# Who issues the eight V weight pieces of a memory-attention kernel, SyncE or ScalarE, with a newly searched instruction order

## The chip, the cores and the metric

The kernel runs on one core of a Trainium2 chip. Its time is device time in microseconds (us) from launch to end; runs of one kernel are compared by their median. A difference is written as after minus before, so a positive number means slower. The engines are TensorE (PE), VectorE (DVE), ScalarE (ACT), GpSimd (POOL) and SyncE (SP); SP, ACT and POOL can each issue DMAs.

## The reference

Four layers run one after another on 2048 tokens of width 512, in bfloat16: attention with memory, a gated feed-forward layer, and both once more, each behind a layer norm and added to its input. The attention walks over 64 segments of 32 tokens. Eight memory rows stand ahead of each segment, and the first eight output rows of a segment are the memory of the next, so that segments form a chain.

```python
for s in range(n_seg):                      # 64 segments of 32 tokens
    h = concat([mem, x[:, s*32:(s+1)*32]])  # 8 + 32 rows, 512 wide
    q, k, v = h @ Wq, h @ Wk, h @ Wv        # 32 heads of 128
    p = softmax(mask(q k^T * scale))
    o = (p v) @ Wo
    mem, out = o[:, :8], o[:, 8:]
x = x + attention(layernorm(x))
x = x + (sigmoid(xn w_gate) * (xn w_up)) w_down
# both lines a second time with the same weights
```

## The kernel before

**Stages.** `Kern.trace` records the whole kernel as tasks. A step (`emit_step`) handles one segment of the first attention layer together with the segment six steps earlier of the second, 70 steps in all; a block is four segments. V does not depend on the chain except for the memory rows, so it is computed ahead for whole blocks (`v_group`, `v_pass`, `v_half`, `v_strip`): a token block of x is loaded (`load_x`), normalised on VectorE with one power function on GpSimd (`layernorm_T`), transposed on TensorE (L595), copied to a tile `xvf` or `xvl` by ScalarE or VectorE, and multiplied by the V weights `wv_sb` (L635, L673, L762). The product is copied from PSUM to SBUF (L1228 on ScalarE, L1230 on VectorE) and written by a DMA to a scratch tensor `scr` in HBM, from which each step reads its V rows back (`vsb`).

**The start.** While the weights of 16 MB are on their way, TensorE does V work for the first blocks. The V weights come in eight pieces of 512 KB (`load_weights`, L511), one for each four heads; then the pieces of `wq_sb`, `wk_sb` and `wo_sb`, between which stand the loads of x and the writes to `scr`. Until the first transposed block is there, TensorE runs filler products on a tile `hot` (L1214), which are part of no result.

**The order.** The string `SEQUENCE` holds a packed order of all tasks and, for each task that two engines may do, the engine. `Planner.plan` unpacks it, and `replay` walks through it with estimated durations, from which it picks buffers, the number of filler products and the place up to which TensorE must have come before a large feed-forward weight load is issued (`pace`). Within each engine the instructions then stand in that order, and each waits by semaphores for what it needs.

**What the V pieces wait for, before.** All eight are issued by SyncE. A piece carries a dependency on the piece two ahead of it (`tk.after`), so that two are under way at a time. Apart from that the framework beneath gives each DMA of SyncE (and of ScalarE) one of eight semaphores in turn, here called lanes; a DMA that takes a lane waits until the DMA that had it last has landed.

Of the kernel before, what the change touches and what calls it, by code (L numbers as in the profile page):

```python
# [1293 lines left out]
```

## Time and profile before

| what | value |
|---|---|
| timed runs | 1745.2, 1745.24, 1746.65 us; median 1745.24 us |
| profiled execution, first to last instruction | 1747.1 us |
| TensorE busy | 1733.4 us (99%) |
| VectorE, ScalarE, GpSimd busy | 1248.4, 1128.5, 859.0 us |
| DMA, mean | 156 GB/s, 273.41 MB |
| chain that ended last | TensorE 94%, DMA 3% |

The span of the profiled execution, its own time, lies 1.9 us (0.1%) above the median of the timed runs; the page shows no time around it. A difference that is worked out in the trace is therefore put on the median as it is. On the page, the idle time of an engine counts only where the chain of waits passes through it; TensorE is busy nearly throughout, so what can change the time is where TensorE stands idle or runs filler, and that is at the two ends.

### The profile page before, as it was taken

To read this page: it belongs to the slowest core of one execution; us is meant where nothing else is said; L and a number is where in the kernel's file an instruction comes from. 1 tells how busy PE (TensorE), PEld (TensorE's weight loads), DVE (VectorE), ACT (ScalarE), POOL (GpSimd) and SP (SyncE) were. 2 spreads that over 40 slices of the span, in tenths; PEclk is the share of its full clock that TensorE was granted. 3 is DMA by queue.
4 is the path that set the end of the run, shared out by engine and by line. 5 is a ranking of instruction groups with operands and counts; after the bars stand their busy time and mean duration, and the time that the engine had idled before them with its cause. 6 is when DMAs were issued, how large, how long until landed. Compare 5 with 4: busy or idle time off the path is not lost.

```text
span 1747.1 us, 91842 instructions
## 1 busy us (share of the span) xinstructions
PE 1733.4 (99%) x39162; PEld 1491.8 (85%) x39162; DVE 1248.4 (71%) x4208; ACT 1128.5 (65%) x3119; POOL 859.0 (49%) x1367
## 2 busy tenths in 40 slices
PE   9999999999999999999999999999999999999998
PEld 4688789889898988989888888989888888988886
DVE  5677777677767776786777767776777776767676
ACT  3576777566666766666666666666665666666564
POOL 5624345635544554445445554544455364454543
PEclk9999999999999999999999999999999999999999
DMA  8935355645645555545555464545455464554644
GB/s 285 320 100 155 109 151 161 195 113 153 174 130 163 156 159 143 165 125 164 152 148 158 136 184 128 166 138 153 132 174 166 139 174 128 144 156 131 178 120 134
DMA packets 145583, 273.41 MB, mean 156 GB/s; under 512 B 39686, under 2 KB 86018, under 8 KB 145174
## 3 DMA queue, kind: packets, MB, share of 16 engines
q0 software_dynamic: 72944, 198.79, 39.8%
q1 hardware_dynamic: 72230, 68.75, 13.3%
q8 instruction: 307, 5.03, 1.2%
q14 instruction: 102, 0.84, 0.2%
HBM read 221.78 MB, written 27.07 MB: 142 GB/s over the span
## 4 chain that ended last, share of the span: by engine, by line
PE 94%; DMA 3%; DVE 1%; SPq 1%; issue 1%; POOL 0%; ACT 0%; POOLq 0%; ACTq 0%
PE bank L868 34%; PE bank L995 17%; PE bank L1097 12%; PE bank L762 8%; PE bank L635 6%; PE bank L1120 6%; PE bank L904 4%; PE bank L976 4%; PE bank L950 2%; PE bank L595 1%; PE bank L1214 1%; DMA wk_sb<-in_A_Wk_dram 1%; DMA wo_sb<-in_A_Wo_dram 0%; PE bank L1065 0%; DMA scr<-wu 0%
## 5 line engine op out<-in xcount | busy, mean ns | idle before, releaser
L868 PE MATMUL bank<-hT,wq_sb 128*128 128x80 bf16 (+3 forms) x8960 | 616.4, 198 | 1.0 <-DVE hT L1008 0.3
L868 PE MATMUL bank<-hT,wk_sb 128*128 128x80 bf16 (+3 forms) x8960 | 616.3, 198 | 0.8 <-DMA wk_sb<-in_A_Wk_dram 0.6
L1228 ACT CAST qku<-bank 128x480 bf16<-128x480 f32 (+4 forms) x770 | 384.7, 508 | 223.7 <-PE bank L868 194.6
L868 PEld LDWEIGHTS <-wq_sb 128*128 128x128 bf16 x8960 | 454.2, 99 | 32.1 <-issue 15.1
L868 PEld LDWEIGHTS <-wk_sb 128*128 128x128 bf16 x8960 | 446.9, 99 | 1.1 <-DMA wk_sb<-in_A_Wk_dram 0.7
L995 PE MATMUL bank<-otsb,wo_sb 128*128 128x80 bf16 (+1 forms) x8960 | 360.2, 198 | 2.2 <-DMA wo_sb<-in_A_Wo_dram 1.3
L918 DVE TENSOR_TENSOR st<-bank,cst 40x240 f32<-40x240 f32 (+3 forms) x768 | 280.5, 368 | 113.2 <-PE bank L904 97.5
L995 PEld LDWEIGHTS <-wo_sb 128*128 128x128 bf16 x8960 | 336.6, 99 | 15.5 <-DMA wo_sb<-in_A_Wo_dram 2.0
L1228 ACT CAST otsb<-bank 128x480 bf16<-128x480 f32 (+3 forms) x420 | 200.2, 483 | 83.4 <-PE bank L976 52.8
L1090 POOL DMA_DIRECT2D wu<-in_B_w_up_dram x217 | 166.5, 768 | 170.0 <-PE bank L950 36.4
L1114 POOL DMA_DIRECT2D wd<-in_B_w_down_dram x217 | 156.9, 723 | 182.0 <-PE bank L1120 39.6
L1224 POOL DMA_DIRECT2D vsb<-sst x351 | 178.2, 512 | 129.6 <-ACT sst L1228 64.7
L1089 POOL DMA_DIRECT2D wg<-in_B_w_gate_dram x217 | 166.4, 767 | 138.1 <-PE bank L1097 56.7
L928 ACT ACTIVATE st<-st 80x240 f32<-80x240 f32 (+3 forms) x420 | 159.2, 381 | 58.0 <-DVE st L925 54.8
L1097 PE MATMUL bank<-xnT,wg 128*128 128x128 bf16 (+2 forms) x1784 | 171.5, 218 | 0.0
L1097 PE MATMUL bank<-xnT,wu 128*128 128x128 bf16 (+2 forms) x1784 | 171.1, 218 | 0.0
L930 DVE TENSOR_REDUCE small<-st 80x6 f32<-80x240 f32 (+3 forms) x420 | 151.5, 363 | 23.4 <-ACT st L928 20.2
L1220 ACT ACTIVATE ptsb<-bank,small 120x160 bf16<-120x160 bf16 (+3 forms) x430 | 156.6, 386 | 17.2 <-PE bank L950 10.7
L904 PE MATMUL bank<-qku 128*128 128x80 bf16 (+1 forms) x2240 | 162.7, 197 | 1.0 <-issue 0.9
L925 DVE TENSOR_TENSOR st<-st,small 80x240 f32<-80x240 f32 (+3 forms) x420 | 155.0, 370 | 5.7
L939 DVE TENSOR_TENSOR pb<-st,small 80x240 bf16<-80x240 f32 (+3 forms) x420 | 154.1, 370 | 5.7
L923 DVE TENSOR_REDUCE small<-st 80x6 f32<-80x240 f32 (+3 forms) x420 | 152.5, 364 | 6.2
(108 smaller groups left out, 2554.1 us busy)
## 6 DMA issues: line engine op xcount, KB each, us to landing
wg<-in_B_w_gate_dram POOLq DMA_DIRECT2D x220, 256.0 KB, 4.2
wu<-in_B_w_up_dram POOLq DMA_DIRECT2D x220, 256.0 KB, 4.2
wd<-in_B_w_down_dram POOLq DMA_DIRECT2D x220, 256.0 KB, 3.9
vsb<-scr SPq DMA_DIRECT2D x137, 66.0 KB
scr<-vst SPq DMA_DIRECT2D x90, 96.0 KB
vsb<-scr POOLq DMA_DIRECT2D x93, 66.0 KB, 3.4
vsb<-sst SPq DMA_DIRECT2D x179, 32.0 KB
vsb<-sst POOLq DMA_DIRECT2D x169, 32.0 KB, 2.8
```

What stands on the lines that cost most here:

```text
L868: nc.tensor.matmul(o_ap, lhsT=W[:, c, h * P:(h + 1) * P], rhs=mv(c), start=(c == 0), stop=(c == DC - 1))
L904: nc.tensor.matmul(s_all(SB)[:, w0 + i, :], lhsT=fview(qku[:, i, 0, 0:1], [(1, P)]), rhs=qku[:, i, 1, 0:ncol], start=True, stop=True)
L918: pl.add("DVE", dve_ns(n, True), lambda gsz=gsz, hs=hs, st=st, SB=SB, pj_=pj_, npj_=npj_, mk=mk, idx=idx: nc.vector.tensor_tensor(out=st[p ...
L928: pl.add("ACT", act_ns(n), lambda hs=hs, st=st: nc.scalar.activation(out=st[pr, hs], in_=st[pr, hs], func=ACTF.Exp, scale=self.scale), r=s ...
L995: nc.tensor.matmul(WB[:, c * ncol:(c + 1) * ncol], lhsT=self.wo[:, h, c * P:(c + 1) * P], rhs=otsb[:, hl, 0:ncol], start=(h == 0 and c == ...
L1089: pl.add("POOL", 760, lambda wg=wg, fs=fs: nc.gpsimd.dma_start(out=wg[:], in_=self.wgv[:, :, fs]), r=[("wo", self.H - 1)], w=[gk] + bt, la ...
L1090: pl.add("POOL", 760, lambda wu=wu, fs=fs: nc.gpsimd.dma_start(out=wu[:], in_=self.wuv[:, :, fs]), r=[("wo", self.H - 1)], w=[uk] + bt, la ...
L1097: nc.tensor.matmul(gu[:, 2 * i + k, 0:n], lhsT=W[:, c, i * P:(i + 1) * P], rhs=xnT[:, c, rw], start=(c == 0), stop=(c == DC - 1))
L1114: pl.add("POOL", 760, lambda wd=wd, ip=ip: nc.gpsimd.dma_start(out=wd[:], in_=self.wdv[:, 2 * ip:2 * ip + 2, :]), w=[dk] + (["boot"] if se ...
L1220: nc.scalar.activation(out=dst, in_=src, func=ACTF.Copy, scale=by)
L1224: {"SP": nc.sync, "POOL": nc.gpsimd}[tk.on].dma_start(out=got[1], in_=got[2])
L1228: nc.scalar.copy(out=dst, in_=src)
```

## The change

- The V weight pieces, and the pieces of Wq, Wk and Wo, may be issued by SyncE or by ScalarE; a bit in the packed order says which. In the order given, ScalarE issues all eight V pieces, ahead of its table load, and one piece each of Wk and Wq later.
- The dependency of a V piece on the piece two ahead of it is gone.
- The planner's estimate of transfers has a separate bus for each issuing engine, eight lanes for SyncE and eight for ScalarE, other constants, and a table load of 1240 ns before ScalarE's first computing task.
- `SEQUENCE` is another order of the whole kernel. TensorE's products are the same in number apart from the filler (58 filler products before, 56 after; the first batch 23 before, 18 after).

```diff
-    BUS, BUS0, SLOW, BIG, ROOM, TAIL = 345.0, 290.0, 18000.0, 300000, 1.0, 1200.0
-    LEAD = {"SP": 1000.0, "POOL": 1800.0}
-    FIRST = {"PE": 0.0, "ACT": 2040.0, "DVE": 980.0, "POOL": 3500.0, "SP": 750.0}
+    BUS, BUS0, SLOW, BIG, ROOM, TAIL = 335.0, 304.0, 20400.0, 300000, 1.0, 1850.0
+    TAILP, CP, STEAL, FIX = 1000.0, 142.0, 0.4, 12400.0
+    LEAD = {"SP": 600.0, "ACT": 600.0, "POOL": 2800.0}
+    FIRST = {"PE": 0.0, "ACT": 800.0, "DVE": 980.0, "POOL": 3500.0, "SP": 750.0}
+    TABLE = 1240.0
...
+            if e == "ACT" and not tk.nb and not table:
+                table, t = True, max(t, free[e] + self.TABLE)
...
-            if e == "SP":
-                lanes.append(tk.done)
-                if len(lanes) >= 8:
-                    free[e] = max(end, lanes[-8])
+            if e == "SP" or e == "ACT" and tk.nb:
+                lanes[e].append(tk.done)
+                if len(lanes[e]) >= 8:
+                    free[e] = max(end, lanes[e][-8])
...
-        def ld(dst, src, nb, keys, after=()):
-            return pl.add("SP", 480, lambda: nc.sync.dma_start(out=dst, in_=src), r=after, w=keys, boost=self.boot(), lat=1750.0, nb=nb)
+        def ld(dst, src, nb, keys, after=(), engs=("SP", "ACT")):
+            return pl.add(engs, {e: 480 for e in engs}, lambda: ("dma", dst, src), r=after, w=keys, boost=self.boot(), lat=1750.0, nb=nb)
...
-            tk = ld(self.wv[:, :, cs], wv_v[:, :, cs], P * self.DC * n * P * 2, [("wv", h) for h in range(h0, h0 + n)], [("wv", h0 - 8)] if h0 > 4 else [])
-            if h0 > 4:
-                tk.after = pl.writer[("wv", h0 - 8)]
+            ld(self.wv[:, :, cs], wv_v[:, :, cs], P * self.DC * n * P * 2, [("wv", h) for h in range(h0, h0 + n)])
...
-                    {"SP": nc.sync, "POOL": nc.gpsimd}[tk.on].dma_start(out=got[1], in_=got[2])
+                    {"SP": nc.sync, "ACT": nc.scalar, "POOL": nc.gpsimd}[tk.on].dma_start(out=got[1], in_=got[2])
```

In the built program the first DMAs of the two issuing engines stand as follows, in program order, each with its lane and with the DMA whose landing it waits for (the lanes go round over both engines' DMAs together):

```
 1 ACT wv piece 1   lane 0                     13 ACT wv piece 5   lane 4, waits for 5
 2 SP  x (xs3)      lane 1                     14 SP  mask 3 KB    lane 5, waits for 6
 3 SP  x (xs4)      lane 2                     15 ACT wv piece 6   lane 6, waits for 7
 4 SP  x (hff)      lane 3                     16 SP  mem0 8 KB    lane 7, waits for 8
 5 SP  x (xs0)      lane 4                     17 SP  x (xa1)      lane 0, waits for 9
 6 ACT wv piece 2   lane 5                     18 SP  x (xs1)      lane 1, waits for 10
 7 SP  x (xs2)      lane 6                     19 ACT wv piece 7   lane 2, waits for 11
 8 SP  x (xa0)      lane 7                     20 SP  wq 393 KB    lane 3, waits for 12
 9 SP  x (xs5)      lane 0, waits for 1        21 SP  x (oxT)      lane 4, waits for 13
10 ACT wv piece 3   lane 1, waits for 2        22 ACT wv piece 8   lane 5, waits for 14
11 SP  x (oxT)      lane 2, waits for 3        23 SP  x (xs3)      lane 6, waits for 15
12 ACT wv piece 4   lane 3, waits for 4        24 SP  x (hff)      lane 7, waits for 16
```

After its eighth piece ScalarE's stream goes on with the table load, then the copies of the first two transposed blocks to `xvf` (two copies, both on ScalarE; before, one of the two was VectorE's), for which the first V product waits.

208 lines of the change are left out of this document (110 added, 98 removed).

## The prediction

> **What bounds the kernel now.** I read the page first, then a table of stretches, then the timeline of TensorE with the waits ahead of its rows, and last the queue of SyncE at the start. The page:
>
> ```profile
> span 1747.1 us, 91842 instructions
> PE 1733.4 (99%) x39162; PEld 1491.8 (85%) x39162; DVE 1248.4 (71%) x4208; ACT 1128.5 (65%) x3119; POOL 859.0 (49%) x1367
> ```
>
> TensorE is idle for only 13.7 us. Where those lie says the table of stretches (length, then busy time of PE, PEld, DVE, ACT and POOL, then granted clock, DMA share, GB/s):
>
> ```profile
> core 0: us, PE busy (x) PEld busy (x) DVE busy (x) ACT busy (x) POOL busy (x), PEclk, DMA share, GB/s
> 0.00:10.00 10.00, 8.94 (x36) 3.71 (x36) 4.04 (x12) 1.59 (x2) 3.65 (x19) 1.00 0.70 214
> 10.00:20.00 10.00, 10.00 (x54) 4.67 (x52) 6.76 (x19) 4.06 (x8) 5.95 (x14) 1.00 0.87 283
> 20.00:40.00 20.00, 17.64 (x119) 8.04 (x118) 11.26 (x28) 7.72 (x19) 12.75 (x25) 1.00 0.93 311
> 40.00:60.00 20.00, 19.79 (x310) 11.67 (x309) 10.90 (x34) 9.25 (x24) 15.06 (x29) 1.00 1.02 373
> 60.00:80.00 20.00, 18.12 (x324) 11.95 (x320) 12.53 (x42) 11.96 (x40) 8.83 (x18) 1.00 0.97 310
> 100.00:1700.00 1600.00, 1597.06 (x36638) 1401.08 (x36635) 1159.64 (x3925) 1056.84 (x2897) 784.22 (x1218) 1.00 0.53 150
> 1700.00:1747.00 47.00, 41.88 (x1089) 33.61 (x1085) 30.39 (x106) 22.33 (x79) 19.12 (x28) 1.00 0.47 134
> ```
>
> From 100 to 1700 us TensorE misses 2.9 us. No new order can win more than that there, and the end has 5.1 us idle, most of it the last additions and the output's landing. So the first 80 us decide; there the DMA engines are nearly full and TensorE waits for weights. TensorE's timeline (start, length, row; in brackets the idle time ahead and what ended it):
>
> ```profile
> 1.06 7.77 PE L1214 MATMUL bank<-hot 128*128 128x512 bf16 x23 [1.06 <-DVE cst L484]
> 8.67 0.39 PE L595 MATMUL bank<-cst,xn 128*128 128x128 bf16 x4
> 9.50 0.76 PE L1214 MATMUL bank<-hot 128*128 128x512 bf16 x3
> 10.23 2.76 PE L635 MATMUL bank<-wv_sb,xvf 128*128 128x512 bf16 x12
> 20.79 2.76 PE L635 MATMUL bank<-wv_sb,xvf 128*128 128x512 bf16 x12 [0.45 <-DMA wv_sb<-in_A_Wv_dram]
> 25.69 1.04 PE L635 MATMUL bank<-wv_sb,xvf 128*128 128x512 bf16 x4 [1.91 <-DMA wv_sb<-in_A_Wv_dram]
> 57.05 0.27 PE L868 MATMUL bank<-hT,wq_sb 128*128 128x54 bf16 x4 [0.21 <-DMA wq_sb<-in_A_Wq_dram]
> 62.06 0.27 PE L868 MATMUL bank<-hT,wk_sb 128*128 128x54 bf16 x4 [0.56 <-DMA wk_sb<-in_A_Wk_dram]
> 68.99 0.47 PE L995 MATMUL bank<-otsb,wo_sb 128*128 128x40 bf16 x12 [0.22 <-DMA wo_sb<-in_A_Wo_dram]
> 77.49 0.47 PE L995 MATMUL bank<-otsb,wo_sb 128*128 128x40 bf16 x12 [0.49 <-DMA wo_sb<-in_A_Wo_dram]
> 78.58 0.84 PE L995 MATMUL bank<-otsb,wo_sb 128*128 128x40 bf16 x20 [0.62 <-DMA wo_sb<-in_A_Wo_dram]
> ```
>
> The first V product starts at 10.23. Two waits for V pieces cost 0.45 + 1.91 = 2.36 us, five for the later weights 0.21 + 0.56 + 0.22 + 0.49 + 0.62 = 2.10 us. After that TensorE is full, so what the start loses or wins goes through to the end. SyncE's queue and its neighbours show why the pieces are late:
>
> ```profile
> 0.81 0.46 SPq L511 DMA_DIRECT2D wv_sb<-in_A_Wv_dram  x1
> 1.33 0.96 SPq L724 DMA_DIRECT2D xs<-in_A_x_dram  x2
> 2.34 0.43 SPq L511 DMA_DIRECT2D wv_sb<-in_A_Wv_dram  x1
> 4.51 0.38 SPq L511 DMA_DIRECT2D wv_sb<-in_A_Wv_dram  x1
> 8.59 0.40 SPq L511 DMA_DIRECT2D wv_sb<-in_A_Wv_dram  x1
> 18.17 0.40 SPq L511 DMA_DIRECT2D wv_sb<-in_A_Wv_dram  x1
> ```
>
> The third piece is issued when the first has landed (4.51), the fourth when the second has (8.59), and the eighth only at 18.17.
>
> **The waits that are left.** The change takes out the dependency between pieces, but the built program still has a wait ahead of six of the eight: the lanes go round over the DMAs of SyncE and ScalarE together, while the planner counts eight for each. Pieces 3 to 7 wait for x blocks. Piece 8 waits for the small mask copy, which SyncE issues only when piece 2 has landed. ScalarE works in order, so its table load and the copies of the first transposed blocks stand behind all of that:
>
> ```profile
> 0.81 1.28 ACT L1228 ACT_TABLE_LOAD   x1 [0.81 <-PEq L1275]
> 9.70 0.48 ACT L1228 COPY xvf<-bank 128x384 bf16<-128x384 bf16 x1 [7.61 <-PE bank L595]
> 4.86 0.69 DVE L582 BATCH_NORM_STATS2 small<-xs 128x6 f32<-128x512 bf16 x1 [3.85 <-DMA xs<-in_A_x_dram]
> ```
>
> **Term 1, the first V product.** Piece 2 now has six x blocks and piece 1 beside or ahead of it: 6 x 0.13 + 2 x 0.52 = 1.84 MB. At the 214 GB/s of the first ten microseconds this is down at 8.6. From 4.51, when 0.52 MB was down, to 8.59, when 1.31 MB was, the rate was 0.79 / 4.08 = 193 GB/s; this gives 4.51 + 1.32 / 0.193 = 11.3. I take 9.9, the middle. Then the mask copy. No row shows it; the nearest are small transfers of GpSimd's queue, in the whole run and in the first 80 us (KB, median us to landing):
>
> ```profile
> vsb<-sst POOLq DMA_DIRECT2D x169, 32.0 KB, 2.8
> vsb<-scr POOLq DMA_DIRECT2D x5, 16.0 KB, 5.3
> ```
>
> I take 3.2, near the lower one, because SyncE's queue then holds only two x blocks ahead of it. Then come piece 8's issue (0.40), the table load (1.28), the copy of 0.48, the second copy (a third as large, some 0.3 with its start) and some 0.1 of handing over: 2.6 us. So the first V product starts at 9.9 + 3.2 + 2.6 = 15.7, between 8.6 + 2.8 + 2.6 = 14.0 and 11.3 + 5.3 + 2.6 = 19.2. Against 10.23 that is **+5.5 us** (+3.8 to +9.0). Nothing covers it: TensorE works in order, and behind these products stands everything else. The earlier x (six blocks ahead of most V pieces; the first one was waited for until 4.86) gives nothing, since the transposed blocks then wait for ScalarE.
>
> **Term 2, the clock.** With 5 fillers fewer in the first batch (18 for 23, so about 1 us less) the last filler ends near 9 where it now ends at 10.2, and TensorE then stands idle for nearly 7 us. What that does to it these rows show: fillers at the start, and the end of the run.
>
> ```profile
> 1.06:6.50 5.44, 5.44 (x13) 1.90 (x14) 1.00 0.80 240
> 6.57:8.83 2.26, 2.26 (x11) 0.88 (x9) 1.00 0.94 324
> 1743.60:1747.30 3.70, 0.06 (x1) 0.00 (x0) 0.70 (x1) 0.00 (x0) 0.00 (x0) 1.00 0.13 35
> 1747.30:1749.00 1.70, 0.00 (x0) 0.00 (x0) 0.00 (x0) 0.00 (x0) 0.00 (x0) 0.51 0.00 0
> ```
>
> The first 13 fillers take 5.44 us (0.42 each), the next 11 2.26 us (0.21 each): a cold start costs 13 x 0.21 = 2.7 us. After TensorE's last product the granted clock stays 1.00 for 3.7 us and is then 0.51. An idle time of 7 us is longer than that, so I count a second cold start, **+2.7 us** (0 if the clock holds, 2.7 at the most as the rows go). The Trainium skill, "TensorE: Matmul & The Clock Gate", part 1 on the HAM clock gate, says that a window of about 3.4 us without work halves the clock and that a busy window of that length restores it; the trace agrees on the first (3.7 us). By the page's window the restart would cost half of 3.4, 1.7 us, an estimate from that page, and the sum 1 us less; the measured 5.44 us decide.
>
> **Term 3, the two V waits.** From 15.7 on the pieces lie ready: the last is issued near 13.5 and in the trace of before a piece takes 3.7 to 7.5 us to land (0.81 to 4.51, 18.17 to 25.69), so by 21, while the built order asks for it only after some 12 us of V products. **-2.4 us.** If a piece still is late, part of it stays.
>
> **Term 4, the later weights.** The built order puts SyncE's first write of V results behind 13 us of V products and its last before the big weight pieces behind 19 us. Ahead of the first stand 6.3 MB, down near 22 us at the 214 and 283 GB/s of the table. So the transfers pause until the V results come, at 15.7 + 2.7 + 13 = 31 us, and run freely from 15.7 + 2.7 + 17 = 35.4 on. From there 15.1 MB remain up to the last piece of `wo_sb`: at 373 GB/s 40.5 us, at 310 GB/s 48.7 us, so until 76 to 84. TensorE asks for that piece after 60 us of products, which by the idle-free pace of before takes 61.4 us: at 79.8. So TensorE waits 0 to 4 us there, beside 2.10 now. I take the 2.1 again: **0** (-2.1 to +2.3).
>
> The rest of the order (steps, feed-forward loads, end) I cost at nothing: 2.9 us of idle time in 1600 leave nothing to take, and the built order asks for the feed-forward weights at least 5.7 us of products after their release, before 5.9. That cover gone, some tenths of a microsecond each time; I allow 1.5 us either way.
>
> **Sum.** 5.5 + 2.7 - 2.4 + 0 = +5.8 us. The span of the profiled execution would go from 1747.1 to 1752.9, the median from 1745.24 to **1751.0 us**.
>
> **Rivals.** (a) *It does what it says*: the pieces leave back to back. Then ScalarE is done with them at 0.81 + 8 x 0.4 = 4.0 and with its table at 5.3, long before the first copy. With the x blocks ahead the second lands about 1 us sooner, the first V product starts near 9.3 (-0.9), and the waits of 2.36 and 2.10 go: -5.4 us, 1739.9 us. It decides if piece 2 and the mask copy are down before about 6 us. For it speaks that the DMA share was 0.70 and 0.87 in the first 20 us, room for about 1 MB more; against it the waits in the built program. The Trainium skill, "DMA: Bandwidth & Descriptors", section "Issuing engines are not separate DMA queues", says that issuing from several engines saves only issue time, which speaks against this rival; no run here shows it yet. (b) *The late start is absorbed*: the first V product at the lower end, 14.0 (+3.8), a cold start of 2.7, -2.4, and the 2.1 of later waits gone because the weights get ahead: +2.0, 1747.2 us. (c) *The transfers become the bound*: the upper ends of terms 1 and 4, 9.0 + 2.7 - 2.4 + 2.3 = +11.6, 1756.8 us; the share of 1.02 from 40 to 60 us speaks for it.
>
> **How the numbers follow.** The median of three runs tells about 0.2%, 3.5 us, from no change. The forecast has 0.55, (a) 0.10, (b) 0.23, (c) 0.12. Faster is (a) alone: 0.10. Within 0.2% (to 1748.7) are most of (b) and the lower edge of the forecast: 0.25. Slower: 0.65. The forecast's own range is 1747.5 to 1754.5. The range for 8 in 10 leaves out (a) and the upper part of (c): 1744 to 1756.
>
> **What would show it.** In the trace after: ScalarE's table load starts near 13.5 instead of 0.81; the third and later V pieces have gaps between them; TensorE is idle from about 9 to 15.7; the first V products are 0.43 us apart and later 0.21; no waits for `wv_sb`; waits of about 2 us for `wk_sb` and `wo_sb` before 85 us. A table load before 6 us, or a first V product before 11, makes the prediction wrong at term 1; products at full speed after the pause, at term 2; TensorE idle time in 100 to 1700 us far from 3 us, in what I costed at nothing.

## The result, and the profile after

| | runs | median, us | lowest to highest |
|---|---|---|---|
| before | 6 | 1745.9 | 1744.1 to 1751.54 |
| after | 6 | 1757.32 | 1755.54 to 1758.42 |

After is slower by a factor of 1.0061 (95% interval 1.005 to 1.0072), which is 10.6 us (8.7 to 12.6). The forecast was slower by 5.8 us, 1751.0 us, between 1744 and 1756; the measured median lies 1.3 us above that range. The profiled execution of after took 1755.54 us, its span is 1753.7 us. (One execution further down, of the run e16, took 2863.2 us at a granted clock of 0.556; it is left out of that run's median and ratio.) From the page of after:

```profile
span 1753.7 us, 91577 instructions
PE 1721.8 (98%) x38946; PEld 1492.5 (85%) x39160; DVE 1256.8 (72%) x4187; ACT 1139.6 (65%) x3140; POOL 874.6 (50%) x1407
```

TensorE seems to have lost 12 us of busy time, but it shows 38946 products for 39160 weight loads: some 200 records of products are missing in this trace. A second profile of the same kernel (the run e10 below) has them from 100 to 1700 us; there TensorE is busy for 1597.45 of 1600 us, where before has 1597.06:

```profile
100.00:1700.00 1600.00, 1597.45 (x36668) 1402.71 (x36665) 1165.64 (x3900) 1069.23 (x2922) 795.91 (x1251) 1.00 0.53 150
```

So in that execution the loss is ahead of 100 us. The table of stretches of after (columns as in the prediction):

```profile
10.00:20.00 10.00, 4.06 (x10) 1.45 (x11) 3.44 (x11) 2.53 (x4) 1.54 (x3) 0.66 1.10 345
20.00:30.00 10.00, 9.95 (x56) 4.90 (x56) 6.36 (x18) 5.76 (x17) 3.91 (x8) 1.00 0.21 66
40.00:80.00 40.00, 35.29 (x475) 20.32 (x478) 22.49 (x66) 17.29 (x49) 29.87 (x56) 1.00 0.98 339
```

From 10 to 20 us TensorE works 4.06 us, at a granted clock of 0.66. From 20 to 30 us the DMA engines all but stop (share 0.21, 66 GB/s); before has them full there:

```profile
20.00:30.00 10.00, 7.64 (x64) 3.30 (x63) 5.63 (x15) 4.83 (x11) 5.10 (x11) 1.00 1.01 342
```

From 40 to 80 us TensorE stands idle for 4.7 us (2.1 in before). Its timeline in after names the causes:

```profile
8.47 0.54 PE L1228 MATMUL bank<-hot 128*128 128x512 bf16 x2
15.94 4.67 PE L649 MATMUL bank<-wv_sb,xvf 128*128 128x512 bf16 x12 [6.92 <-ACT xvf L1242]
20.44 0.61 PE L609 MATMUL bank<-cst,xn 128*128 128x128 bf16 x8
49.58 0.27 PE L882 MATMUL bank<-hT,wq_sb 128*128 128x54 bf16 x4 [0.71 <-DMA wq_sb<-in_A_Wq_dram]
56.46 0.27 PE L882 MATMUL bank<-hT,wk_sb 128*128 128x54 bf16 x4 [0.63 <-DMA wk_sb<-in_A_Wk_dram]
61.61 0.28 PE L882 MATMUL bank<-hT,wk_sb 128*128 128x54 bf16 x4 [1.18 <-DMA wk_sb<-in_A_Wk_dram]
67.03 0.27 PE L882 MATMUL bank<-hT,wq_sb 128*128 128x54 bf16 x4 [1.39 <-DMA wq_sb<-in_A_Wq_dram]
70.15 0.27 PE L882 MATMUL bank<-hT,wk_sb 128*128 128x54 bf16 x4 [0.53 <-DMA wk_sb<-in_A_Wk_dram]
```

The first V product starts at 15.94, after 6.92 us without work, and waits for ScalarE's copy `xvf`. The twelve products take 20.44 - 15.94 = 4.50 us; with the clock at full speed they take 2.60 (from 9.90 to 12.50 in e1 below). No wait for `wv_sb` is left; five waits for `wq_sb` and `wk_sb` make 4.44 us. ScalarE's queue, and two rows of SyncE's:

```profile
0.81 12.94 ACTq L1238 DMA_DIRECT2D wv_sb<-in_A_Wv_dram  x8
13.77 1.28 ACT L1242 ACT_TABLE_LOAD   x1 [13.77 <-DMA wv_sb<-in_A_Wv_dram]
15.07 0.82 ACT L1242 COPY xvf<-bank 128x384 bf16<-128x384 bf16 x2
```

```profile
7.78 0.92 SPq L509 DMA_DIRECT2D cst<-cst  x1
31.53 1.41 SPq L1238 DMA_DIRECT2D scr<-wu  x2
```

The eight pieces occupy ScalarE's queue from 0.81 to 13.75, not back to back; the last is issued at 13.37, when the mask copy, issued at 7.78, has landed (13.35). Then come the table load and the two copies. SyncE's first write of V results, behind which the next weights of its queue stand, leaves at 31.53. Up to 40 us after has issued three pieces of `wq_sb` and `wk_sb`, before seven.

### The profile page after: what moved, and what is told of

It is laid out like the page before. It is cut to its first block, busy times and chain, and to the rows that moved or that the text cites. A ratio compares the mean times of both kernels' runs of the same rounds, so it can differ in the third digit from the quotient of the medians.

```text
span 1753.7 us, 91577 instructions
## 1 busy us (share of the span) xinstructions
PE 1721.8 (98%) x38946; PEld 1492.5 (85%) x39160; DVE 1256.8 (72%) x4187; ACT 1139.6 (65%) x3140; POOL 874.6 (50%) x1407
## 4 chain that ended last, share of the span: by engine, by line
PE 89%; DMA 4%; DVE 3%; issue 1%; ACT 1%; POOL 1%; SPq 0%; ACTq 0%; POOLq 0%; DVEq 0%
PE bank L882 32%; PE bank L1009 17%; PE bank L1111 11%; PE bank L776 7%; PE bank L649 6%; PE bank L918 4%; PE bank L990 4%; PE bank L1134 4%; PE bank L964 2%; PE bank L609 1%; DVE st L932 1%; DMA wk_sb<-in_A_Wk_dram 1%; DMA wu<-in_B_w_up_dram 1%; DMA wo_sb<-in_A_Wo_dram 0%; DMA vsb<-scr 0%
## 5 line engine op out<-in xcount | busy, mean ns | idle before, releaser
L1242 ACT CAST qku<-bank 128x480 bf16<-128x480 f32 (+3 forms) x770 | 382.4, 506 | 205.4 <-PE bank L882 181.5
L1009 PE MATMUL bank<-otsb,wo_sb 128*128 128x80 bf16 (+1 forms) x8960 | 355.9, 198 | 0.8
L1238 POOL DMA_DIRECT2D vsb<-sst x361 | 182.4, 509 | 197.4 <-ACT sst L1242 82.5
L1234 ACT ACTIVATE ptsb<-bank,small 120x160 bf16<-120x160 bf16 (+4 forms) x442 | 162.0, 384 | 16.3 <-PE bank L964 9.8
L944 DVE TENSOR_REDUCE small<-st 80x6 f32<-80x240 f32 (+3 forms) x420 | 151.7, 363 | 26.1 <-ACT st L942 23.9
L1238 POOL DMA_DIRECT2D vsb<-scr x197 | 104.8, 533 | 114.0 <-PE bank L990 55.6
L918 PE MATMUL bank<-qku 128*128 128x80 bf16 (+1 forms) x2240 | 158.5, 198 | 1.1
```

The costliest lines, as they stand in the source:

```text
L918: nc.tensor.matmul(s_all(SB)[:, w0 + i, :], lhsT=fview(qku[:, i, 0, 0:1], [(1, P)]), rhs=qku[:, i, 1, 0:ncol], start=True, stop=True)
L1009: nc.tensor.matmul(WB[:, c * ncol:(c + 1) * ncol], lhsT=self.wo[:, h, c * P:(c + 1) * P], rhs=otsb[:, hl, 0:ncol], start=(h == 0 and c == ...
L1234: nc.scalar.activation(out=dst, in_=src, func=ACTF.Copy, scale=by)
L1238: {"SP": nc.sync, "ACT": nc.scalar, "POOL": nc.gpsimd}[tk.on].dma_start(out=got[1], in_=got[2])
L1242: nc.scalar.copy(out=dst, in_=src)
```

## The experiments

Each run was timed beside before; `before` in the table is the median of its runs in the same series. The ratio is not the quotient of the two medians; where they differ, the text gives both. The theory at the outset was the prediction's: ScalarE comes free late, which delays the first V product and cools the clock. The first rival was that the new order costs something by itself.

| run | first V product, us | its median | before beside it | ratio (95% interval) |
|---|---|---|---|---|
| e1 before again | 9.90 | 1746.72 | 1749.1 | 0.9995 (0.9986 to 1.0004) |
| e2 old order, ScalarE issues | 12.01 | 1750.59 | 1749.1 | 1.0007 (0.9997 to 1.0017) |
| e3 new order, SyncE issues | 9.50 | 1755.75 | 1749.1 | 1.0041 (1.0027 to 1.0055) |
| e4 new order, joined pieces | 10.19 | 1753.97 | 1749.1 | 1.0042 (1.0028 to 1.0056) |
| e10 after again | 15.08 | 1758.73 | 1748.4 | 1.0068 (1.0054 to 1.0081) |
| e5 first copies on VectorE | 10.92 | 1752.47 | 1748.4 | 1.0025 (1.0016 to 1.0033) |
| e7 fillers in the pause | 16.28 | 1759.57 | 1748.4 | 1.0067 (1.0054 to 1.0081) |
| e9 weights ahead of V writes | 15.73 | 1754.34 | 1748.4 | 1.0035 (1.0023 to 1.0048) |
| e6 table load early | 17.37 | 1759.46 | 1748.76 | 1.0054 (1.0041 to 1.0068) |
| e8 old order, joined pieces | 9.38 | 1746.59 | 1748.76 | 0.9987 (0.9977 to 0.9996) |
| e11 e4 and e9 together | 10.15 | 1749.68 | 1748.76 | 1.0007 (0.9993 to 1.002) |
| e12 old order, a copy on VectorE | 9.15 | 1748.0 | 1748.76 | 0.9993 (0.9982 to 1.0003) |
| e16 e8 again | 9.17 | 1748.01 | 1746.86 | 1.0001 (0.9992 to 1.0011) |

**e1, before again.**

> The kernel before, run and profiled again. Theory (the prediction's trace sums are right and were put on a profiled execution that lay high): single runs scatter over some 1744 to 1751 us with a median of 1745 to 1746.5, and a new profile has a span near 1743 to 1745 instead of 1747.1, with fewer waits for weights before 80 us. Rival (a profiled execution is a typical one): span again 1747 +- 0.7, and the 10.6 us between the medians then hold some 4 us that the two traces do not show.

The span came as the theory said, the medians did not: 1746.72 us here and 1749.1 for before beside it. Single runs of this one program go from 1744.5 to 1752.5 us. The new profile has a span of 1744.4 and a time of 1746.13 us, 1.7 more than its span. Its waits for V pieces are shorter than those of the first profile (0.85 us for 2.36):

```profile
9.90 2.76 PE L635 MATMUL bank<-wv_sb,xvf 128*128 128x512 bf16 x12
12.50 0.61 PE L595 MATMUL bank<-cst,xn 128*128 128x128 bf16 x8
20.52 2.76 PE L635 MATMUL bank<-wv_sb,xvf 128*128 128x512 bf16 x12 [0.50 <-DMA wv_sb<-in_A_Wv_dram]
23.86 0.82 PE L635 MATMUL bank<-wv_sb,xvf 128*128 128x512 bf16 x3 [0.35 <-DMA wv_sb<-in_A_Wv_dram]
```

The spans of 91 executions of before are on record, in all series together: 1742.6 to 1752.1 us, median 1746.1. So the profiled execution on which the forecast stood (1747.1) lay 1.0 us above the middle, and the new one 1.7 below it.

**e2, the issuer alone, in the old order.**

```diff
+    for tk in self.vpieces: tk.on = "ACT"          # and no tk.after
+    order = self.vpieces + [tk for tk in order if tk not in self.vpieces]
```

> The order of before, with only the issuer changed: the eight V pieces stand ahead of everything else in ScalarE's queue, the waits of one piece for the one before the last are gone. Theory (what counts is when ScalarE comes free): six pieces still wait for a lane, the last for the small memory block, so ScalarE is done with them at 9 to 11 us, the first V product starts at 11.5 to 13.5 (before 10.2), the pause is too short for a cold clock, the 2.4 us of waits for V pieces go: 1744.5 to 1748. Rival A (the new order is what costs): the same or faster, at most 1746. Rival B (two queues in each other's way cost by themselves): 1751 or more.

```profile
10.18 1.28 ACT L1232 ACT_TABLE_LOAD   x1 [10.18 <-DMA wv_sb<-in_A_Wv_dram]
```

```profile
12.01 2.76 PE L636 MATMUL bank<-wv_sb,xvf 128*128 128x512 bf16 x12 [2.74 <-ACT xvf L1232]
```

In the trace it is as expected: ScalarE is held until 10.18, the first V product is 2.1 us later than in e1, and the waits for V pieces are gone. In the time the two nearly cancel (1.0007, 1.5 us by the medians). The median of 1750.59 lies above the 1748 expected, as before's own in this series does (1749.1). The move of the issuer is not what costs 10 us.

**e3, the issuer undone, in the new order.**

```diff
+    for tk in piece: tk.on = "SP"
+    # v = V piece, . = the next other DMA of SyncE, as in before
+    lead = [sp.pop(0) if q == "." else piece.pop(0) for q in "v..v..v.v.vv.v....v"]
+    order = lead + [tk for tk in order if tk not in lead]
```

> The order of after, with the eight V pieces issued by SyncE again, between its x blocks as in before. Theory (ScalarE behind the pieces is what costs): the table load is at 0.8 us, the first V product near 10.5, no cold clock, some 2 us of waits for V pieces come back, 2 to 4 us for later weights stay: 1746 to 1750. Rival A (the new order of the other 1700 us is what costs): 1754 or more although the first V product is early.

```profile
9.50 2.76 PE L650 MATMUL bank<-wv_sb,xvf 128*128 128x512 bf16 x12 [0.15 <-ACT xvf L1249]
19.06 0.40 PE L610 MATMUL bank<-cst,xn 128*128 128x128 bf16 x4 [2.33 <-DVE xn L601]
59.84 0.28 PE L883 MATMUL bank<-hT,wq_sb 128*128 128x54 bf16 x4 [1.29 <-DMA wq_sb<-in_A_Wq_dram]
```

My theory fell here. The first V product is as early as before, and still 0.41% (7.2 us) is lost: a block of x is late (2.33 us), and the waits for weights stay. In the new order something costs that has nothing to do with ScalarE. How much is not clean: the late block of x may come from the edit, which sets V pieces between the x blocks. And the profiled execution, the slowest of the five (1757.66), loses some 3 us only at its end, by a stop of 1.47 us ahead of 1738.15 and a granted clock of 0.50 for the 3.4 us behind it.

**e4, nearly back to back.** The eight pieces as four transfers, which the lanes hold only until 7.6 us.

```diff
+    first, n_ = {h: (g[0], len(g)) for g in ((0,), (4,), (8, 12), (16, 20, 24, 28)) for h in g}[h0]
+    # one transfer of n_ pieces at the first of a group, none at the others
```

> The order of after, the eight V pieces on ScalarE joined to four transfers of 1, 1, 2 and 4 pieces, so that the lanes hardly hold them up (the last waits for one x block, near 7.5 us). Theory: table load near 8 us, first V product at 9.5 to 10.5, no cold clock, no waits for V pieces unless the last big transfer is late (0 to 1.5 us), waits for later weights 1 to 4.4 us: 1744 to 1750, so 7 to 13 us below after. Rival A (the new order costs the rest): first V product early, but 1752 or more. Rival B (the transfers are the bound): waits for weights take over, 1753 or more.

```profile
10.19 1.04 PE L653 MATMUL bank<-wv_sb,xvf 128*128 128x512 bf16 x4 [1.23 <-ACT xvf L1246]
12.18 3.21 PE L653 MATMUL bank<-wv_sb,xvf 128*128 128x512 bf16 x8 [0.96 <-DMA wv_sb<-in_A_Wv_dram]
```

The first product is early, as the theory said, but 0.42% is still lost (1753.97 for the 1744 to 1750 expected); again a part of the loss is elsewhere. The DMA engines are still not full from 20 to 30 us (share 0.62, 189 GB/s), and the waits for `wq_sb` and `wk_sb` are 3.5 us. So the theory became: two causes, ScalarE's late start and weights that stand too late in the queues.

**e10, after again.** No edit.

> The changed kernel, run again beside before on one chip, since single runs of before have shown 1744 to 1752.5 us. Theory: the loss is in the first 100 us of the trace (late V start, cold clock, weights later) and comes to 7 to 9 us; the rest of the order adds at most 1. So 7 to 10 us above the median of before measured beside it. Rival (the 10.6 us of the first comparison is the typical loss, and 3 us of it lie outside the first 100 us): 10 to 12 us above.

1.0068 is 11.9 us, by the medians 10.3: the rival's figure. Its profiled execution was the fastest of five (1754.47; the others 1758.1 to 1762.2), so the traces seen so far showed the milder runs of after.

**e5, the first two copies on VectorE.**

```diff
+    for tk in xvf:        # ScalarE's first two copies
+        tk.on = "DVE"
+        order.remove(tk)
+        order.insert(1 + max(order.index(self.pl.tasks[d]) for d in tk.deps), tk)
```

> After, with the first two copies of transposed x (for the first V products) on VectorE instead of ScalarE, each put right behind its transposes; the eight pieces stay on ScalarE with their waits. Theory (ScalarE's queue ahead of these copies makes the first V product late): first V product at 9.5 to 10.5 instead of 15.9, no cold clock; then TensorE stops once for the V results' copies that ScalarE still does after 15 us (0 to 2.5 us). 4 to 7 us below after. Rival (late pieces or the mask copy themselves hold the products): first product still after 14 us, time as after.

```profile
10.92 2.76 PE L649 MATMUL bank<-wv_sb,xvf 128*128 128x512 bf16 x12 [1.96 <-DVE xvf L1249]
16.39 2.76 PE L649 MATMUL bank<-wv_sb,xvf 128*128 128x512 bf16 x12 [1.39 <-ACT xvf L1247]
```

With the pieces and their waits as in after, the first V product starts 4 to 5 us earlier, and TensorE stops once more for ScalarE at 16.39. That is 1.0025 for 1.0068, 7.5 us less (6.3 by the medians). What stands behind the pieces in ScalarE's queue is one cause; the pieces themselves came early enough.

**e7, fillers in the pause.**

```diff
+    third = [tk for tk in order if tk.idx in fill][2]
+    fill[third.idx] = (fill[third.idx][0], fill[third.idx][1] + 120)
```

> After, with 30 more filler matmuls in the pause before the first V product (6.4 us at 0.213 us each). Theory (the cold clock costs 1.9 us, by 12 products in 4.50 us instead of 2.60): granted clock 1.0 from 10 to 20 us, first V product still at 15.5 to 16.2, 12 products in 2.6 us, 1 to 2 us below after. The prediction's price was 2.7. Rival (what is won there is lost at the later weights, since the transfers set the pace): the waits for wq and wk grow by as much, and the time stays within 0.7 us of after.

```profile
10.00:20.00 10.00, 9.13 (x50) 4.18 (x48) 3.39 (x11) 3.38 (x6) 1.54 (x3) 1.00 1.10 345
```

```profile
16.28 2.76 PE L649 MATMUL bank<-wv_sb,xvf 128*128 128x512 bf16 x12 [0.87 <-ACT xvf L1244]
54.50 0.27 PE L882 MATMUL bank<-hT,wk_sb 128*128 128x54 bf16 x4 [1.11 <-DMA wk_sb<-in_A_Wk_dram]
60.27 0.28 PE L882 MATMUL bank<-hT,wk_sb 128*128 128x54 bf16 x4 [1.80 <-DMA wk_sb<-in_A_Wk_dram]
66.69 0.28 PE L882 MATMUL bank<-hT,wq_sb 128*128 128x54 bf16 x4 [2.40 <-DMA wq_sb<-in_A_Wq_dram]
```

The clock stays at 1.00 and the products are fast, yet the time is that of after (1.0067 for 1.0068), as the rival said. Each of the two ratios is known to 2.3 us either way, though, so that a gain of 1 to 2 us is not excluded. Beside e10 the trace shows the gain lost again at the weights: the waits for them are 5.3 us for 3.3, the same weight load of the program (number 240, fillers not counted) starts 1.4 us earlier, and number 400 0.4 us later. But e10 is the mildest of the five profiles of after. Beside the other four, number 1000 still starts 1.3 to 2.3 us earlier, and e7 loses behind that, with 5.5 us of idle time from 100 to 1700 us for 2.6 in e10. So the cold clock is real, and what it costs in the time stays open.

**e9, weights ahead of the V writes.**

```diff
+    early = [tk for tk in order if tk in self.qk_pieces][1:5]
+    for tk in early: tk.on = "SP"; order.remove(tk)
+    order[at:at] = early       # behind SyncE's x blocks, ahead of its first write to scr
```

> After, with the next four pieces of the wq and wk weights put on SyncE's queue ahead of its first write of V results, so that they fill the pause of the transfers from 20 to 30 us (66 GB/s). Theory (that pause is what makes the weights late): the DMA share from 20 to 30 us rises from 0.21 to 0.6 or more, the waits for wq and wk fall from 4.4 us to 0.5 to 2.5, first V product unchanged near 15.9; 2 to 4 us below after. Rival (the transfers between 40 and 80 us are full and set the waits): the waits move to other pieces, wo among them, and the time stays within 1 us of after.

```profile
20.00:30.00 10.00, 10.00 (x57) 4.85 (x55) 6.74 (x21) 6.13 (x16) 4.46 (x9) 1.00 0.83 265
40.00:80.00 40.00, 38.71 (x563) 22.94 (x562) 24.22 (x71) 19.00 (x56) 29.01 (x55) 1.00 1.02 353
```

The first V product is as late as in after (15.73), the pause is filled (0.83 for 0.21), TensorE's idle time from 40 to 80 us falls from 4.7 to 1.3 us, and the time from 1.0068 to 1.0035, 5.8 us (4.4 by the medians). That is more than the 3.2 us of waits for weights that are gone between these two traces, but weight load number 1000 starts 2.7 to 5.5 us earlier than in the five profiles of after, 4.5 on the mean. The place of four transfers in a queue is worth half of the whole loss.

**e11, both causes taken away.** The edits of e4 and e9 together.

> The order of after with both causes taken away: the V pieces joined to four transfers as in the run before with that, and the four wq and wk pieces ahead of the first V write. Theory (late start and late weights are the whole loss, and the rest of the new order costs nothing): first V product near 10.2, waits for wq and wk up to 2 us, within 2 us of before. Rival (the gains do not add, or the new order costs by itself): 3 us or more above before.

```profile
20.00:30.00 10.00, 9.95 (x76) 4.52 (x76) 8.13 (x23) 6.32 (x17) 7.08 (x15) 1.00 0.96 315
```

1.0007, with an interval that holds 1 and ends 3.5 us above before. The rest of the new order costs nothing that this can measure.

**e6, the table load early.**

```diff
+    if tk is self.vpieces[0]:                     # the second piece in the order
+        nc.scalar.copy(out=self.spare, in_=self.negh[:])
```

> After, with one tiny ScalarE copy behind the second V piece, so that the table load (1.28 us) lies in the queue's first wait and not between the last piece and the first copies. Theory (transfers now set the pace, the start is partly hidden): first V product 1.3 us earlier, at 14.6, and of that 0.4 to 1.3 us in the time. Rival (the start is on the path in full): 1.3 to 2 us below after; beside before 8.5 to 10 us above.

```profile
1.84 1.28 ACT L1248 ACT_TABLE_LOAD   x1 [1.84 <-issue]
5.60 10.85 ACTq L1240 DMA_DIRECT2D wv_sb<-in_A_Wv_dram  x6
```

Neither. One more instruction in ScalarE's queue dealt the lanes anew: the seventh piece now waits for the mask copy and the eighth until 16.08, so the first V product starts at 17.37. The price of the table load stays open. By the medians it lies 10.7 us above before (1.0054, 9.4 us), as after does: 2.3 us more in the start than in e10, or 1.3 to 1.4 more than in the other four profiles of after, are not to be seen in the time.

**e8 and e16, e12: what the issuer is worth in the old order.** e8 joins the pieces as e4 does; e12 is e2 with ScalarE's first copy on VectorE, by the edit of e5.

> The order of before, with the V weights issued by ScalarE ahead of its other work as four transfers of 1, 1, 2 and 4 pieces, which the lanes hold up to some 6 us at most: what the change says, without its order. Theory (with ScalarE free by 6 us the move of the issuer costs nothing and the waits for V pieces go): first V product at 9.5 to 10.3, waits for V pieces 0 to 1 us instead of 0.9 to 2.4, later weights as in before: 0.5 to 2.5 us below before. Rival (four long transfers push the x blocks back): TensorE waits for xn, and the time is up to 2 us above before.

> The order of before with the V weights issued by ScalarE as four transfers of 1, 1, 2 and 4 pieces, run again because its gain is small (0.9987, 0.9977 to 0.9996). Theory (the waits for V pieces are worth 1 to 2.4 us and nothing takes their place): 1 to 3 us below before, ratio 0.998 to 0.9995. Rival (a chance result): within 0.7 us of before.

> The order of before with the eight V pieces at the head of ScalarE's queue, as in the run that changed only the issuer, and the one early copy of transposed x that stood behind them (2.74 us of waiting there) on VectorE. Theory: first V product at 9.5 to 10.3, no waits for V pieces, later weights as in before: 1 to 3 us below the run with the issuer alone, 0 to 2.5 us below before. Rival (ScalarE's other copies, held until 11 us, stop TensorE instead): as the run with the issuer alone, 1 us above before.

```profile
5.94 1.28 ACT L1235 ACT_TABLE_LOAD   x1 [5.94 <-DMA xs<-in_A_x_dram]
```

```profile
9.38 2.92 PE L639 MATMUL bank<-wv_sb,xvf 128*128 128x512 bf16 x12
```

In e8 ScalarE has its table load at 5.94, the first V product starts at 9.38, and no wait for V pieces is left. The first series gave 2.3 us less than before, the second none (1.0001); together they show no gain. e12 starts at 9.15 and is within its interval of before. No version beat before beyond doubt.

**e13, e14, e15: after three times more.** No edit. They took 1757.56, 1757.83 and 1759.75 us.

> The changed kernel, profiled again. Its two profiled executions so far (1755.5 and 1754.5 us) were the fastest of their series, whose medians are 1757.3 and 1758.7. Theory (the slow executions are late in the same places): an execution near 1758 shows its extra 2 to 4 us before 100 us, as a later first V product (16 to 17.5) or longer waits for wq and wk, and nothing new after 200 us. Rival (something else in the 1600 us behind): the first 100 us as in the two profiles, the extra time in waits for feed-forward weights or V rows.

> As the look before it, the changed kernel once more: theory, an extra 2 to 4 us in an execution near 1758 lies before 100 us (first V product at 16 to 17.5, or waits for wq and wk over 4.5 us); rival, it lies behind 200 us.

> As the two looks before it, the changed kernel once more: theory, an extra 2 to 4 us in an execution near 1758 lies before 100 us (first V product at 16 to 17.5, or waits for wq and wk over 4.5 us); rival, it lies behind 200 us.

The slowest, e15 (span 1758.0):

```profile
16.06 5.30 PE L649 MATMUL bank<-wv_sb,xvf 128*128 128x512 bf16 x12 [7.01 <-ACT xvf L1242]
21.15 1.00 PE L609 MATMUL bank<-cst,xn 128*128 128x128 bf16 x8
63.10 0.36 PE L882 MATMUL bank<-hT,wk_sb 128*128 128x54 bf16 x4 [2.48 <-DMA wk_sb<-in_A_Wk_dram]
```

Its first product comes 1.0 us after that of e10, and one wait for `wk_sb` alone takes 2.48 us, behind which the clock is at 0.50 once more, from 62.9 to 66.3. Weight load number 1000 starts at 95.59 us in e15 and at 92.81 in e10, +2.8; at load number 5000, near 250 us, it is +4.4, at the last +5.3. For e13 and e14 it is +2.1 and +2.3 at number 1000 and +3.1 and +3.4 at the last. So two thirds of the extra lie ahead of 100 us, as the theory said, or half in e15; the rest is in single delays behind that, some of them within 250 us, that I did not trace to a cause. One of them every profile of after has: TensorE stops near 160 us without a wait that the profile shows, for 0.49 us in e10, 0.73 to 0.78 in three and 1.41 in e15; in e7 that stop takes 2.27 us. The five spans of after are 1752.7 to 1758.0, their mean 1755.3; those of before 1747.1 and 1744.4, mean 1745.8. The difference of the means, 9.5 us, agrees with the timed 10 to 12, and so do the medians of all the spans on record: 1756.2 for 14 executions of after and 1746.1 for 91 of before, 10.1 us.

## Why the prediction was right or wrong

**What bounds the kernel.** Right in the main: from 100 to 1700 us TensorE works 1597.06 us in before and 1597.45 in e10. The slower executions of after lose another 1.0 to 2.5 us behind 100 us (e13 to e15, beside e10).

**The lanes.** Right: six pieces wait, the last for the mask copy; table load at 13.77 (forecast near 13.5), gaps between the pieces, first V product late.

**Term 1**, +5.5: 15.94 - 10.23 = +5.7. The sum held because two errors cancelled: piece 2 landed at 7.70, not 9.9, and the mask copy took 13.35 - 7.78 = 5.57 us, not 3.2; the upper row of the two that I had (5.3) was the nearer one.

**Term 2**, +2.7: over the first twelve products 4.50 - 2.60 = 1.9 us in the first profile, 2.4 to 2.5 in the four others (in e15, 21.15 - 16.06 - 2.60). Counted until the clock is back, 3.9 to 5.9 us at half speed, it is 1.9 to 2.9 us, 2.6 on the mean, so the size was right. The estimate from the Trainium skill, "TensorE: Matmul & The Clock Gate", part 1, was 1.7: below every profile. Whether it belongs in the sum stays open: e7 takes the cold clock away and no gain is seen in the time, but one of 1 to 2 us would not be seen either.

**Term 3**, -2.4: the waits are gone, but they were 0.85 us in the second profile of before. The size of the term was that of one execution.

**Term 4**, 0: this is the step that failed. The pause was forecast (from 22 us to SyncE's first write at 31; it was 31.53), and then costed at nothing, by one sum of bytes up to the last piece of `wo_sb` at 79.8. The waits came earlier, from 49.58 to 70.15, for `wq_sb` and `wk_sb`: 4.44 us for 2.10, +2.3 in that trace. In the five profiles of after the waits for weights are 3.1 to 4.5 us, in the two of before 2.10 and 1.49: +2.1 on the mean, where the sum has 0. To set four of these pieces ahead of the pause (e9) gains 4.4 to 5.8 us in the time. A date for each piece was needed, not one for the last. Two slips are in its working besides. At 214 and then 283 GB/s the 6.3 MB would be down at 24.7 us, not 22 (in after the transfers ran out near 20.5, at 345 GB/s). And the free run is counted from 17 us of V products where the sentence ahead of it says 19; from 19 it would begin at 37.4, and the wait be 0 to 6.3 us instead of 0 to 4.

**The sum and the median.** The span was forecast at 1752.9 and was 1753.7. That it came so near is luck. The terms of these two traces give 5.7 + 1.9 - 2.4 + 2.3 = 7.5, and the traces differ by 6.6; but this execution of after lies 2.5 us below the median of its spans, and that of before 1.0 above its own. From median to median the spans differ by 10.1 us. On the mean of the five profiles of after and the two of before the terms are +5.7 (first V product), +2.6 (clock), -1.6 (V waits) and +2.1 (later weights), 8.8 of the 9.5 us between the mean spans. Beside the forecast's +5.8, 2.1 us are missing at term 4 and 0.8 at term 3. Then the forecast took the span of before as the time of that execution and put the difference on the median. But a time is 1.6 to 2.1 us longer than its span in all the executions on record, so that execution took some 1749 us, nearly 4 above the median it was put on. That median, 1745.24 of three runs, lay low: the later medians of before are 1746.7 to 1749.1.

**Rivals.** (a), that it does what it says, needs free lanes; where they are free (e8, e16, e11) the result is before's time, not 5.4 us less. The page that spoke against it, the Trainium skill, "DMA: Bandwidth & Descriptors", section "Issuing engines are not separate DMA queues", agrees with e2, e8, e12 and e16: in the old order the issuer moved the time by -0.13% to +0.07%. (b) did not occur. (c) is nearest in time (1756.8) and right that the weights become the wait, but not by a first product at 19.2.

**What stays open.** What a table load costs there; what the cold clock costs in the time; what the delays behind 100 us in the slower runs of after are; and how the transfers' lateness splits between the order of the queues and the later start, since the two overlap (e5 alone gives 7.5 us, e9 alone 5.8, and e11, with the joined transfers of e4 beside e9, all of it).

## What to carry to other kernels

A DMA put on a computing engine's queue brings its waits along: what counts is what stands behind it on that engine, and a wait that no line of the kernel asks for can come from semaphores shared between queues. When a start becomes later, date every transfer behind it and not only the last, and don't take it that delays which lie one behind another on the same stretch add up: test one with the other left in place. Before a trace is set against a median, find out by how much executions of the same program differ.

## What the runs showed of the hardware

- A copy of a 40x40 block inside SBUF took 4.8 (e10) to 6.0 us (e7) to land while the DMA engines were full (share 1.11 in after, from its issue to its landing).
- The clock fell to 0.50 after much shorter pauses than the 3.7 us seen before. In e5 a wait of 1.86 us ahead of 55.71 was enough:

```profile
56.00:57.00 1.00, 1.00 (x41) 0.93 (x37) 0.24 (x1) 0.24 (x1) 0.82 (x2) 1.00 1.08 387
57.00:58.00 1.00, 1.00 (x4) 0.36 (x3) 0.00 (x0) 0.12 (x1) 0.87 (x3) 0.50 1.11 313
```

It stayed there until about 60.4 us. In e4 two pauses of 1.23 and 0.96 us did the same, and in e11 pauses of 1.19 and 0.97 us did not. The Trainium skill, "TensorE: Matmul & The Clock Gate", part 1, puts the drop after an idle window of some 3.4 us; in e5 it came with TensorE at work both within the 3.4 us and right ahead of it.
- Within one trace the granted clock changes only at distances that are whole multiples of 3.41 us. In after it falls at 13.00 and is back at 19.83, which these rows enclose:

```profile
12.00:13.00 1.00, 0.00 (x0) 0.00 (x0) 0.98 (x3) 0.00 (x0) 0.00 (x0) 1.00 1.11 342
13.00:14.00 1.00, 0.00 (x0) 0.00 (x0) 0.49 (x4) 0.23 (x1) 0.40 (x1) 0.50 1.10 346
19.00:20.00 1.00, 1.00 (x4) 0.34 (x3) 0.00 (x0) 0.43 (x1) 0.00 (x0) 0.59 1.10 344
20.00:21.00 1.00, 1.00 (x12) 0.74 (x11) 0.00 (x0) 0.29 (x2) 0.00 (x0) 1.00 0.58 188
```

In the stretch of 3.41 us right ahead of the drop TensorE had been idle for 58% in e4 and for 55% in e5; in e11 no such stretch of the start had more than 44%, and the clock stayed. So in these runs it counted how a pause lay in this grid, and not its length alone. The border is not sharp: 56% left the clock up in before (23.61 to 27.02 us). The way back differed too: from the first V product to the full clock it took 3.9 us in after and 4.8 to 5.9 us in the four other profiles of it.
- One more instruction in one engine's queue changed which transfers waited for which, and moved the first V product by 1.3 to 2.3 us (e6).
